# An MLP that begins on two of the first four tiles, with a shorter float64 conversion and column sums on PE

## The chip, the core and the metric

The kernel runs on one core of one Trainium2 chip. The core has five engines with their own instruction queues: PE (TensorE, matrix products), DVE (VectorE), ACT (ScalarE), POOL (GpSimd) and SP (SyncE, which here only issues DMAs). An engine takes its instructions strictly in the order in which they were written for it; between engines they wait on semaphores. The metric is the time of one execution on the device in microseconds, the median of several runs.

## The reference

Three stages follow each other on 4 x 768 = 3072 tokens.

```python
# 1. a state space model: 4 batches, 8 heads, head width 32, state 16
M = (C @ B.T) * exp(cum_i - cum_j) * causal            # in chunks, with a carried state
y = M @ x + (C @ state) * exp(cum)
# 2. an MLP; w_in [256, 2048] and w_out [2048, 256] are float64
x = relu(x @ w_in) ** 2 @ w_out
# 3. eight experts; each token goes to the one with the largest cosine to expert_emb
out[mask] = gate[mask] * (relu(x[mask] @ w1[e]) @ w2[e])   # w1[e] [256, 1024]
```

Products are taken in two float16 pieces per operand (a rounded part and the rest), so each product of the reference is three matmuls. The float64 weights are turned into float32 on the chip by integer operations on their two 32-bit words, then scaled by a power of two that comes from their size, then split into the two pieces.

## The kernel before

The 3072 tokens are 24 tiles of 128, in 6 groups of 4 tiles. Per tile the first stage is a chain: `ssm_b` (PE L655, DVE L663, POOL L671), `ssm_u` (the carried state: POOL L689, PE L694, DVE L701, POOL L707), `ssm_c` (PE L726 and L731, ACT L736), `ssm_d` (PE L746, DVE L752, ACT L759 and L762, and for the second piece DVE L771, or ACT L766 with POOL L768), and a DMA transposition (SP L776) that brings the tile to the MLP's layout.

The MLP works by `unit(u)`: group g = u // 16 and one sixteenth f = u % 16 of the 2048 hidden columns. The first product of a unit is 6 matmuls of 512 columns (four tiles at once, L896), then ReLU on ACT (L901), the square on DVE (L909) or ACT (L906), the rounded piece on ACT (L913) and the rest on DVE (L917) or POOL (L920). The second product is 12 matmuls of 256 columns (L933). All tiles of a group must have gone through the first stage before its first unit starts, and for group 0 also quarter f // 4 of w_in must be converted, scaled and split; a second product needs quarter f // 4 of w_out.

The weights: two matrices (wi = 0, 1) in four quarters of 1024 columns. For each, `top64` takes |high word| on ACT (L422) and clamps it on DVE with a running maximum (L429); `scale64` makes the scale out of the maxima (L440 to L469); `part64` builds the float32 value by one shift of 1024 columns (L480) and two passes of 1024 columns that read the raw words (L483, L486), multiplies by the scale and splits (ACT L505, then DVE L508, or POOL L514 with a scaled copy by ACT L512 or DVE L503). The scale needs the maxima of all four quarters.

After the MLP each group goes through `finish` (a transposition by DMA, the logits on PE L982) and `route` (the expert's choice, the place of each token in its expert's list: PE L1040 to L1047), and its rows are scattered to DRAM. The w1 and w2 of eight experts are loaded and split in the background (ACT L553 and L570, DVE L572). At the end run 28 `job`s, each 128 rows of one expert: a first product of 12 matmuls of 512 columns (L1256), ReLU into two pieces (ACT L1307, DVE L1309), a DMA transposition (SP L1267), a second product of 16 matmuls (L1281, L1283), the gate (ACT L1291, DVE L1294), a scatter by POOL (L1297). Jobs 13 and later use a second table of jobs, which exists only when all tokens are placed.

The order on every engine is written by a list scheduler, `weave`: each stage is a generator that yields an engine and a cost, the scheduler takes the piece that could start first by its own clock, and among nearly equal ones the one with the smallest due number (`DUE`, a table of some hundred numbers). `keep_warm` puts matmuls on zeros (L367) where its clock sees PE idle before the MLP.

## Time and profile before

| | us |
|---|---|
| median of 3 runs | 543.41 (541.89 to 543.64) |
| the profiled execution, time | 545.03 |
| its span, first to last instruction | 543.3 |
| PE busy | 506.5 (93%) |
| DVE busy | 367.2 (68%) |
| ACT busy | 319.6 (59%) |
| POOL busy | 170.1 (31%) |

Read it by stages. Up to 58 us PE works for the first stage of some nine tiles and fills the gaps with matmuls on zeros. From there to 373 us it runs the MLP with the rest of the first stage and the routing in between; from there on the jobs. PE is the engine that is nearly always busy; DVE and ACT are close to it in the first 300 us and half idle in the jobs.

### The profile page before, as it was taken

The page shows a single profiled execution, that of the slowest core. Times are in us where ns is not written, and L with a number is a line of the kernel's source. Part 1 is how long each engine was busy: PE and PEld are TensorE (multiplying, and loading weights), DVE is VectorE, ACT ScalarE, POOL GpSimd, SP SyncE. Part 2 cuts the span into 40 slices and gives each one's busy share as a digit, 9 for nine tenths or more (in the row PEclk, how much of TensorE's full clock was granted, in tenths as well). Part 3 has the DMA queues.
Part 4 walks back from the last instruction along what each step waited for, and adds up shares of the span by engine and source line. Part 5 has one row for each costly group of instructions (what it writes and reads, how often), then busy time and mean ns, then how long its engine had stood idle before and what let it go on. Part 6 is the DMA issues. An engine that isn't in the chain of part 4 may idle for free. (4 is left out here: it accounts for less than half of the span.)

```text
span 543.3 us, 11918 instructions
## 1 busy us (share of the span) xinstructions
PE 506.5 (93%) x4092; PEld 324.8 (60%) x4092; DVE 367.2 (68%) x958; ACT 319.6 (59%) x676; POOL 170.1 (31%) x182
## 2 busy tenths in 40 slices
PE   8788888999999999999998999999898898998993
PEld 6566544667776767676765766666454454554551
DVE  5988698897788798889777687765564332333330
ACT  3645679743898797989888698445422222332330
POOL 0565745536425712500140041040114121121212
PEclk9999889999999999999999999999999999999998
DMA  8933302113622334327139030203898885879751
GB/s 333 408 126 98 108 11 60 49 30 109 190 94 99 116 62 162 112 61 250 53 144 189 7 108 20 31 31 67 166 146 158 167 194 116 160 138 153 147 114 45
DMA packets 116556, 65.64 MB, mean 121 GB/s; under 512 B 105605, under 2 KB 109967, under 8 KB 113424
## 3 DMA queue, kind: packets, MB, share of 16 engines
q1 hardware_dynamic: 114000, 58.46, 43.6%
q0 software_dynamic: 2496, 6.40, 3.7%
q8 instruction: 36, 0.59, 0.4%
q14 instruction: 24, 0.20, 0.1%
HBM read 32.58 MB, written 8.13 MB: 75 GB/s over the span
## 5 line engine op out<-in xcount | busy, mean ns | idle before, releaser
L896 PE MATMUL bank<-work 128*128 128x512 f16 x576 | 142.2, 385 | 1.7 <-DVE work L909 1.5
L933 PE MATMUL bank<-work 128*128 128x256 f16 x960 | 119.2, 275 | 0.0
L933 PEld LDWEIGHTS <-work 128*128 128x128 f16 x960 | 93.3, 99 | 22.8 <-DVE work L917 0.8
L896 PEld LDWEIGHTS <-work 128*128 128x128 f16 x576 | 55.2, 99 | 53.6 <-issue 5.7
L1281 PE MATMUL bank<-wexp,work 128*128 x224 | 74.3, 379 | 6.4 <-DMA work<-work 5.8
L1256 PE MATMUL bank<-wexp,work 128*128 x336 | 76.7, 379 | 2.6 <-DMA work<-work 1.9
L1309 DVE SCALAR_TENSOR_TENSOR work<-bank,work 128x512 f16<-128x512 f32 x56 | 37.8, 689 | 52.1 <-ACT work L1307 49.1
L901 ACT ACTIVATE work<-bank 128x512 f32<-128x512 f32 x96 | 56.5, 593 | 27.5 <-PE bank L896 26.0
L1297 POOL DMA_INDIRECT out<-work x28 | 27.5, 981 | 134.4 <-DVE work L1294 80.5
L909 DVE SCALAR_TENSOR_TENSOR work<-bank,work 128x512 f32<-128x512 f32 x80 | 54.5, 685 | 15.9 <-ACT work L901 15.7
L1307 ACT ACTIVATE work<-bank 128x512 f16<-128x512 f32 x56 | 32.4, 595 | 55.5 <-PE bank L1256 29.6
L913 ACT CAST work<-work 128x512 f16<-128x512 f32 x80 | 48.7, 614 | 21.7 <-DVE work L909 18.9
L1283 PE MATMUL bank<-wexp,work 128*128 x224 | 61.0, 272 | 0.0
L920 POOL TENSOR_TENSOR work<-work 128x512 f16<-128x512 f32 x20 | 26.1, 1303 | 105.3 <-ACT work L913 92.5
L1256 PEld LDWEIGHTS <-work 128*128 128x128 f16 x336 | 32.6, 98 | 39.1 <-issue 2.1
L671 POOL TENSOR_SCALAR_AFFINE_SELECT wexp<-wexp 128x512 f32<-128x512 f32 x48 | 38.2, 795 | 54.5 <-DVE wexp L663 30.4
L917 DVE TENSOR_TENSOR work<-work 128x512 f16<-128x512 f32 x60 | 41.5, 696 | 10.2 <-ACT work L913 9.5
L1291 ACT ACTIVATE work<-bank,work 128x256 f32<-128x256 f32 x28 | 13.3, 474 | 54.7 <-PE bank L1283 51.1
L663 DVE TENSOR_TENSOR wexp<-bank,wexp 128x256 f32<-128x256 f32 x96 | 38.1, 415 | 7.7 <-PE bank L655 3.4
L1281 PEld LDWEIGHTS <-work 128*128 128x128 f16 x224 | 21.8, 98 | 35.5 <-DMA work<-work 9.6
L1294 DVE SCALAR_TENSOR_TENSOR work<-bank,work 128x256 f32<-128x256 f32 x28 | 13.5, 483 | 43.0 <-ACT work L1291 43.0
L1079 POOL DMA_INDIRECT xs<-work x24 | 29.5, 1228 | 33.4 <-DVE work L1075 10.4
(201 smaller groups left out, 759.8 us busy)
## 6 DMA issues: line engine op xcount, KB each, us to landing
work<-in_w SPq DMA_DIRECT2D x8, 1024.0 KB
wexp<-in_w SPq DMA_DIRECT2D x8, 1024.0 KB
wexp<-in_w_in SPq DMA_DIRECT2D x4, 1024.0 KB
wexp<-in_w_out SPq DMA_DIRECT2D x4, 1024.0 KB
wexp<-in_x SPq DMA_DIRECT2D x6, 512.0 KB
wexp<-in_ct SPq DMA_DIRECT2D x6, 256.0 KB
wexp<-in_bc SPq DMA_DIRECT2D x6, 256.0 KB
xs<-work SPq DMA_DIRECT2D x9, 132.0 KB
```

The costliest lines, as they stand in the source:

```text
L663: V.tensor_tensor(mv, ps.rearrange("p (a b) -> p a b", b=32), eg[:, t, n * q:n * q + n].rearrange("p h q -> p (h q)").unsqueeze(2) .to_bro ...
L671: G.affine_select(out=mm, in_=mm, pattern=[[0, 4], [1, P]], compare_op=ALU.is_ge, fill=0.0, base=0, channel_multiplier=-1)
L896: T.matmul(p, win[:, wi, kk, f * P:(f + 1) * P], x[:, xi * 2 + kk], start=(n == 0), stop=(n == 5))
L901: S.activation(r, p, AF.Relu, scale=XK)
L909: V.scalar_tensor_tensor(out=r, in0=p, scalar=XK, in1=r, op0=ALU.mult, op1=ALU.mult)
L913: S.copy(gh, r)
L917: V.tensor_tensor(gl, r, gh, ALU.subtract)
L933: T.matmul(po, gg[:, s], wout[:, wi, f], start=(f == 0 and n == 0 and k % 2 == 0), stop=(f == NF - 1 and n == 2), skip_group_check=True)
L1256: T.matmul(p, xj[i][:, xi * 2 + kk], W[:, bass.ds(e, 1), c0:c0 + 512].rearrange("p a b -> p (a b)"), start=(n == 0), stop=(n == 5))
L1281: T.matmul(po, r[:, f], W[:, bass.ds(e, 1), c0:c0 + 512].rearrange("p a b -> p (a b)"), start=(f == 0), stop=False, skip_group_check=True)
L1283: T.matmul(po[:, 0:DM], r[:, 8 + f], W[:, bass.ds(e, 1), c0:c0 + 256].rearrange("p a b -> p (a b)"), start=False, stop=(f == 7), skip_grou ...
L1309: V.scalar_tensor_tensor(out=rh[:, 1, s], in0=p, scalar=0.0, in1=rh[:, 0, s], op0=ALU.max, op1=ALU.subtract)
```

## The change

It has these parts.

- Group 0 of the MLP is no longer 16 units of 512 columns but 32 half-units, `unit0(f, hf)`, of 256 columns: half 0 takes tiles 0 and 1, half 1 tiles 2 and 3. A half waits for its own two tiles only. The rounded and rest pieces of group 0 stand where they stood before; the second products of half 0 go to bank 2, of half 1 to bank 3.
- The conversion (`conv64`) copies the high word on ACT with a factor 2^-112, shifts it on DVE, and then does two passes per half quarter (512 columns), the first into a PSUM bank, the second from it. The clamp with the running maximum is gone. The scale comes from column sums: PE multiplies a quarter, read as bfloat16, by ones (32 output rows, 2 matmuls of 512 columns per quarter), and DVE takes the maximum of the bank.
- The splits, the squares and the tiles' second pieces are shared out anew: 6 of the 8 quarters' rests on DVE (2 before) and 2 on POOL (6 before); squares on ACT: 24 of 32 halves in group 0 (8 of 16 units before), 12 of 16 units in group 1 (8 before), 32 of 64 in groups 2 to 5 (none before); the second piece of a tile's transposition on ACT and POOL for 16 of 24 tiles (2 before); the rests of group 0 on POOL for 16 of 32 halves (none before).
- In `route` four matmuls that add the running counts become one of 32 columns that reads the counts four times over.
- A job's second product may stand on PE only behind the first product of the job two later. A new kind of request, "order", keeps the order without counting as a wait in the scheduler's clock.
- Tables of the first stage use other banks; the zero matmuls have 176 columns instead of 256; `DUE` has new numbers throughout.

```diff
-XK = 2.0 ** -23
+XK = 2.0 ** -22
-DUE = dict(jm=13.1, r0=571.698, r1=-28.445, r2=3.074, r3=58.399, sv=0.3, ss=0.432, sg=0.924, g0=-0.006, g1=1, g2=0,
+DUE = dict(jm=13.1, r0=941.955, r1=-46.678, r2=-171.439, r3=67.992, sv=0.068, ss=0.348, sg=0.312, g0=-32.82, g1=1,
...
-            while th[3] is not None and th[3][0] in ("need", "mark", "due", "spawn"):
+            while th[3] is not None and th[3][0] in ("need", "order", "mark", "due", "spawn"):
...
-                    th[2] = max(th[2], marks[key])
+                    if kind == "need":
+                        th[2] = max(th[2], marks[key])
...
+    def conv64(wi, q):
         x = wides[wi][:, q]
+        xi = x.bitcast(I32)
         yield "need", ("raw", wi, q)
         yield "S", 0.95
-        S.activation(x, pair(wi, q)[:, :, 1].bitcast(F32), AF.Abs)
...
-        V.tensor_scalar(out=x, in0=x, scalar1=TINY64, scalar2=0.0, op0=ALU.max, op1=ALU.max,
-                        accum_out=mq[:, 4 * wi + q:4 * wi + q + 1])
...
+        S.activation(x, pair(wi, q)[:, :, 1].bitcast(F32), AF.Copy, scale=2.0 ** -112)
+        yield "V", 0.6, "L"
+        V.tensor_scalar(out=xi, in0=xi, scalar1=3, scalar2=None, op0=ALU.logical_shift_left)
...
+        for h in range(2):
+            T.matmul(bank[c][32 * q:32 * q + 32, :], one_b[:, 0:32],
+                     x.bitcast(BF16).rearrange("p (e w) -> p e w", w=2)[:, 512 * h:512 * h + 512, 1],
+                     start=(h == 0), stop=(h == 1), skip_group_check=True)
+        yield "mark", ("nrm", wi, q)
...
+        for h in range(2):
+            s = slice(512 * h, 512 * h + 512)
+            yield "order", ("cv", 8 * wi + 2 * q + h - 1)
+            yield "V", 0.6, (2,), "L"
+            V.scalar_tensor_tensor(out=yi, in0=pair(wi, q)[:, s, 1], scalar=-(1 << 31), in1=xi[:, s],
+                                   op0=ALU.bitwise_and, op1=ALU.bitwise_or)
+            yield "V", 0.6, (2,)
+            V.scalar_tensor_tensor(out=xi[:, s], in0=pair(wi, q)[:, s, 0], scalar=29, in1=yi,
+                                   op0=ALU.logical_shift_right, op1=ALU.bitwise_or)
+            yield "mark", ("cv", 8 * wi + 2 * q + h)
...
+    def unit0(f, hf):
+
+        cols = slice(256 * hf, 256 * hf + 256)
+        p, r = bank[f % 2][:, cols], rbuf[f % 2][:, cols]
...
+        for key in ((hr, f - 2), (hg, f - 2), ("part", 0, f // 4), ("d", 2 * hf), ("d", 2 * hf + 1)):
+            yield "need", key
...
+                T.matmul(p, win[:, wi, kk, f * P:(f + 1) * P], xT[0][:, xi * 2 + kk, cols], start=(n == 0),
+                         stop=(n == 5), skip_group_check=True)
...
+        for key in (("part", 1, f // 4), ("cv", 15), ("nrm", 1, 3), ("inv", 1)):
+            yield "need", key
...
+        for k in range(2):
+            po = bank[2 + hf][:, k * DM:k * DM + DM]
+            s = slice(k * P, (k + 1) * P)
+            for n, (gg, wi) in enumerate(((gh, 0), (gh, 1), (gl, 0))):
+                T.matmul(po, gg[:, s], wout[:, wi, f], start=(f == 0 and n == 0 and k == 0),
+                         stop=(f == NF - 1 and n == 2), skip_group_check=True)
...
-        for k in range(4):
-            T.matmul(pos[:, k * E:k * E + E], onef_s[0:1, :], base[0:1, :], start=False, stop=(k == 3),
-                     skip_group_check=True)
+        T.matmul(pos.rearrange("p (t e) -> p t e", e=E), onef_s[0:1, :],
+                 base[0:1].unsqueeze(1).to_broadcast([1, 4, E]), start=False, stop=True, skip_group_check=True)
...
+        yield "order", ("m1j", min(j + 2, JU - 1))
         yield "need", ("out", j - 2)
-        yield "need", ("m2j", j - 1)
+        yield "order", ("m2j", j - 1)
```

What the change does to the order shows at three places. First, on PE, where the MLP begins. In the kernel before L655 is the ninth tile's `ssm_b`, L746 the sixth tile's `ssm_d`, and L896 the first product of the first unit (six matmuls).

```order
L655 MATMUL bank_67<-wexp 128x128
L655 MATMUL bank_68<-wexp 128x128
L655 MATMUL bank_69<-wexp 128x128
L655 MATMUL bank_70<-wexp 128x128
L746 MATMUL bank_70<-wexp 128x128 x2
L896 LDWEIGHTS work
L896 MATMUL bank_63<-work 128x512
L896 LDWEIGHTS work
```

In the changed kernel L642 is `ssm_b`, L881 the first product of a half-unit; ahead of these rows only four tiles have their L642 and three their `ssm_d`.

```order
L881 MATMUL bank_64<-work 128x256
L881 LDWEIGHTS work
L881 MATMUL bank_64<-work 128x256
L881 LDWEIGHTS work
L881 MATMUL bank_64<-work 128x256
L881 LDWEIGHTS work
L881 MATMUL bank_64<-work 128x256
L881 LDWEIGHTS work
L881 MATMUL bank_64<-work 128x256
L642 MATMUL bank_67<-wexp 128x128
L642 MATMUL bank_68<-wexp 128x128
L642 MATMUL bank_69<-wexp 128x128
```

The first product of the first half-units thus moved ahead of five tiles' `ssm_b`. The first row of a second product (L921) comes after 138 matmuls of L881 (23 of 32 half-units) and eight tiles' `ssm_b`, and right behind the last of the 192 matmuls of L921 PE has placed ten tiles' L642, nine tiles' L718 (`ssm_c`, before L731) and seven tiles' L713 (before L726).

Second, on DVE, where the scale of w_in is made (before: L455 takes the maximum to all partitions, L465 is the scale, L480 and L483 the shift and the first pass over raw words of another quarter).

```order
L455 COPY work<-bank_67 128x1
L463 TENSOR_SCALAR work<-work 128x1
L465 TENSOR_SCALAR work<-work 128x1
L469 TENSOR_SCALAR work<-work 128x1
L276 TENSOR_SCALAR work<-work 128x1
L278 TENSOR_SCALAR work<-work 128x1
L276 TENSOR_SCALAR work<-work 128x1
L278 TENSOR_SCALAR work<-work 128x1
L480 TENSOR_SCALAR work<-work 128x1024
L663 TENSOR_TENSOR wexp<-bank_67,wexp 128x256
L483 SCALAR_TENSOR_TENSOR work<-wexp,work 128x1024
```

In the changed kernel L469 takes the maximum, L473 is the scale, L444 and L447 are the two passes over half a quarter, L496 the split of a quarter, L650 and L739 belong to the first stage (before L663 and L752).

```order
L447 SCALAR_TENSOR_TENSOR work<-wexp,bank_65 128x512
L469 TENSOR_SCALAR work<-bank_64 128x1
L472 TENSOR_SCALAR work<-work 128x1
L473 TENSOR_SCALAR work<-work 128x1
L280 TENSOR_SCALAR work<-work 128x1
L444 SCALAR_TENSOR_TENSOR bank_65<-wexp,work 128x512
L739 TENSOR_TENSOR wexp<-bank_70,wexp 128x256
L650 TENSOR_TENSOR wexp<-bank_69,wexp 128x256
L496 SCALAR_TENSOR_TENSOR work<-work 128x2x512
```

The scale's rows moved from the 77th shown row of DVE to the 57th, and the first split follows it at once. The last of the sixteen L447 is the 133rd.

Third, on DVE, jobs 10 to 15, where the second job table comes in (L1309 and L1358 end the first product of a job, two rows each; L1294 and L1343 end its second product).

```order
L1289 TENSOR_TENSOR work<-work 128x1
L1294 SCALAR_TENSOR_TENSOR work<-bank_69,work 128x256
L1289 TENSOR_TENSOR work<-work 128x1
L1294 SCALAR_TENSOR_TENSOR work<-bank_65,work 128x256
L1289 TENSOR_TENSOR work<-work 128x1
L1294 SCALAR_TENSOR_TENSOR work<-bank_69,work 128x256
L1309 SCALAR_TENSOR_TENSOR work<-bank_63,work 128x512
L1309 SCALAR_TENSOR_TENSOR work<-bank_64,work 128x512
L1309 SCALAR_TENSOR_TENSOR work<-bank_67,work 128x512
L1309 SCALAR_TENSOR_TENSOR work<-bank_68,work 128x512
```

The three second products of jobs 10, 11 and 12 stood side by side ahead of the first products of jobs 13 and 14.

```order
L1338 TENSOR_TENSOR work<-work 128x1
L1343 SCALAR_TENSOR_TENSOR work<-bank_69,work 128x256
L1358 SCALAR_TENSOR_TENSOR work<-bank_63,work 128x512
L1358 SCALAR_TENSOR_TENSOR work<-bank_64,work 128x512
L1338 TENSOR_TENSOR work<-work 128x1
L1343 SCALAR_TENSOR_TENSOR work<-bank_65,work 128x256
L1358 SCALAR_TENSOR_TENSOR work<-bank_67,work 128x512
L1358 SCALAR_TENSOR_TENSOR work<-bank_68,work 128x512
L1338 TENSOR_TENSOR work<-work 128x1
L1343 SCALAR_TENSOR_TENSOR work<-bank_69,work 128x256
```

Now first and second products take turns there, as they did before and after that place in the kernel before.

## Rows read from the trace of the kernel before

**Rows 1.** Stretches of core 0: length, each engine busy, TensorE clock, DMA share, GB/s.

```profile
0.00:58.15 58.15, 47.70 (x590) 35.04 (x591) 45.33 (x119) 30.40 (x62) 28.48 (x43) 1.00 0.65 237
58.15:100.00 41.85, 37.89 (x301) 21.25 (x300) 36.77 (x72) 32.08 (x71) 21.24 (x20) 0.92 0.18 45
100.00:200.00 100.00, 99.58 (x1086) 71.89 (x1084) 83.11 (x230) 73.41 (x177) 49.21 (x56) 1.00 0.35 100
200.00:300.00 100.00, 97.22 (x736) 66.49 (x735) 83.07 (x206) 86.38 (x179) 22.79 (x17) 0.98 0.45 133
```

**Rows 2.** Instruction groups of PE from 0 to 100 us: count, busy us, mean ns.

```profile
L896 PE MATMUL bank<-work 128*128 128x512 f16 x96 | 26.2, 414 | 1.5 <-DVE work L909 1.5
...
L655 PE MATMUL bank<-wexp 32*128 32x128 f32 x192 | 10.1, 299 | 0.8 <-DVE wexp L663 0.5 <-ACT wexp L614 0.3
L731 PE MATMUL bank<-wexp 128*32 128x128 f32 x176 | 7.1, 278 | 0.0
L726 PE MATMUL bank<-wexp 128*128 128x128 f32 x36 | 6.2, 296 | 2.0 <-POOL wexp L707 2.0
L933 PE MATMUL bank<-work,wexp 128*128 128x256 f16 x41 | 5.1, 273 | 0.0
```

**Rows 3.** PE in order of time: start us, us, instruction, count, idle before.

```profile
58.15 2.76 PE L896 MATMUL bank<-work 128*128 128x512 f16 x6
...
87.28 0.73 PE L655 MATMUL bank<-wexp 32*128 32x128 f32 x16
87.94 1.47 PE L896 MATMUL bank<-work 128*128 128x512 f16 x6
89.25 1.47 PE L933 MATMUL bank<-work,wexp 128*128 128x256 f16 x12
90.56 1.46 PE L896 MATMUL bank<-work 128*128 128x512 f16 x6
91.85 0.61 PE L726 MATMUL bank<-wexp 128*128 128x128 f32 x4
92.39 0.64 PE L731 MATMUL bank<-wexp 128*32 128x128 f32 x16
```

**Rows 4.** ACT in order of time, the first split of the weights.

```profile
52.22 2.19 ACT L505 ACTIVATE work<-work 128x1024 f16<-128x1024 f32 x2 [1.20 <-DVE work L465]
```

**Rows 5.** POOL in order of time, two halves of the split.

```profile
55.89 2.13 POOL L514 TENSOR_TENSOR work<-work 128x1024 f16<-128x1024 f32 x1
...
69.86 3.09 POOL L514 TENSOR_TENSOR work<-work 128x1024 f16<-128x1024 f32 x1
```

**Rows 6.** DVE in order of time, one subtraction of the MLP.

```profile
70.88 2.61 DVE L917 TENSOR_TENSOR wexp<-work,wexp 128x512 f16<-128x512 f32 x1
```

**Rows 7.** Instruction groups of DVE from 0 to 100 us, shapes apart.

```profile
L663 DVE TENSOR_TENSOR wexp<-bank,wexp 128x256 f32<-128x256 f32 x48 | 19.2, 415 | 2.4 <-PE bank L655 1.2 <-PE bank L446 0.6 <-ACT wexp L633 0.4
...
L429 DVE TENSOR_SCALAR_CACHE_REDUCE work<-work 128x1024 f32<-128x1024 f32 x8 | 9.7, 1212 | 0.9 <-ACT work L422 0.9
...
L909 DVE SCALAR_TENSOR_TENSOR work<-bank,work 128x512 f32<-128x512 f32 x8 | 5.5, 682 | 1.8 <-ACT work L901 1.8
...
L480 DVE TENSOR_SCALAR work<-work 128x1024 int32<-128x1024 int32 x6 | 4.1, 684 | 0.1
```

**Rows 8.** Instruction groups of ACT from 0 to 100 us, shapes apart.

```profile
L505 ACT ACTIVATE work<-work 128x1024 f16<-128x1024 f32 x5 | 5.4, 1100 | 1.2 <-DVE work L465 1.2
...
L906 ACT ACTIVATE work<-work 128x512 f32<-128x512 f32 x7 | 4.4, 628 | 0.0
...
L736 ACT COPY wexp<-bank 128x256 f32<-128x256 f32 x11 | 4.1, 370 | 8.9 <-PE bank L731 7.2 <-PE bank L655 1.1 <-DVE wexp L663 0.4
```

**Rows 9.** PE in order of time, the expert counts of one group.

```profile
262.20 1.05 PE L1044 MATMUL bank<-work 1*128 1x8 f32 x8
```

**Rows 10.** What PE waited for from 373.5 us: total us, times, longest.

```profile
PE bank L1281 <- DMA work<-work: 5.8, 9, 1.4
PE bank L1256 <- DMA work<-work: 1.9, 1, 1.9
```

More of the change, by code (lines that the diff above doesn't have):

```diff
@@ L343, in weave @@
             cost = th[3][1]
-            if eng == "T" and ("m1", 1) not in marks:
+            if eng == "T" and ("h10", 1) not in marks:
                 keep_warm((s - free[eng]) * (DUE["warm"] if s > 6 else DUE["cold"]))
@@ L354, in weave @@
                 th[2] = s + 4.0
-            elif th[3][-1] == "L" or eng == "G":
-                free["L"] = s + cost
-            elif type(th[3][-1]) is tuple:
-                for b in th[3][-1]:
-                    held[b, eng] = th[2] + XLAT[eng]
+            else:
+                if th[3][-1] == "L" or eng == "G":
+                    free["L"] = s + cost
+                for what in th[3][2:]:
+                    if type(what) is tuple:
+                        for b in what:
+                            held[b, eng] = th[2] + XLAT[eng]
             th[3] = next(th[1], None)
@@ L435, in scale64 @@
+    def scale64(wi, inv_ap):
         sc, m = scw[:, wi:wi + 1], mx[:, wi:wi + 1]
-        mi = mxr[:, wi:wi + 1].bitcast(I32)
         for q in range(4):
-            yield "need", ("nrm" if wi == 1 and DUE["nw"] else "top", wi, q)
-        yield "V", 0.2
-        V.tensor_reduce(out=m, in_=mq[:, 4 * wi:4 * wi + 4], op=ALU.max, axis=AX.X)
-        row = bank[4][0:1, 288:416]
+            yield "need", ("nrm", wi, q)
+        c = 2 * wi + 1
+        yield "V", 0.6, (c,)
+        V.tensor_reduce(out=m, in_=bank[c], op=ALU.max, axis=AX.X)
+        row = bank[c][0:1, 0:P]
@@ L452, in scale64 @@
-        yield "T", 0.1, (4,)
-        T.matmul(bank[4][:, 288:289], onef_s[0:1, :], m[0:1], start=True, stop=True, skip_group_check=True)
-        yield "V", 0.1, (4,)
-        V.tensor_copy(m, bank[4][:, 288:289])
-        if wi == 1 and DUE["nw"]:
-            yield from scale_bits(m.bitcast(I32), sc.bitcast(I32), inv_ap.bitcast(I32), 205)
-            inverses(inv_ap.bitcast(I32), 49)
-            yield "mark", ("scale", wi)
-            yield "mark", ("inv", wi)
-            return
-        yield "V", 0.2
@@ L471, in scale64 @@
+        inverses(hi, -14)
         yield "mark", ("inv", wi)
@@ L644, in ssm_b @@
         yield "need", ("m", t - 1)
-        bs = [(4 if g else 2) + r for r in range(4)]
-        sc = [bank[bs[r]][:, (0, 256)[g > 0 and r > 1]:][:, 0:256] for r in range(4)]
+        bs = [4 + r for r in range(4)]
+        sc = [bank[bs[r]][:, (0, 256)[r > 1]:][:, 0:256] for r in range(4)]
         yield "need", ("ct", g)
@@ L883, in unit @@
         r = rbuf[u % 2]
-        if g == 0:
-            gh, gl = (first[:, 1024 * f + 512 * i:1024 * f + 512 * i + 512] for i in range(2))
-        else:
-            gh, gl = ghb[u % 3], glb[u % 3]
-        for key in (("m1", u - 1), ("r", u - 2), ("part", 0, f // 4), ("eg", 0)):
+        gh, gl = ghb[u % 3], glb[u % 3]
+        if u < NF + 2:
+            for key in (("hr0", u - 2), ("hg0", u - 2)):
+                yield "need", key
+        yield "order", ("m1", u - 1)
+        for key in (("r", u - 2), ("part", 0, f // 4), ("eg", 0)):
             yield "need", key
@@ L921, in unit @@
         yield "mark", ("gl", u)
-        yield "due", DUE["m0"] + DUE["m1"] * u if u < NF else due(u + 2)
-        for key in (("m2", u - 1), ("part", 1, f // 4), ("m", 3)):
-            yield "need", key
+        yield "due", due(u + 2)
+        yield "order", ("m2", u - 1)
         if f == 0:
@@ L1249, in job @@
             yield "need", ("jr%d" % q, j - 2)
-            yield "need", ("m1j", j - 1)
+            yield "order", ("m1j", j - 1)
             yield "T", 1.296, (hb[j % 2][q],)
@@ L1455, in tile_ssm_mlp_moe @@
         th += [(d + DUE["ob"], ssm_b(t)), (d + DUE["ou"], ssm_u(t)), (d + DUE["oc"], ssm_c(t)), (d, ssm_d(t))]
-    for u in range(NF * NGRP):
+    for f in range(NF):
+        for hf in range(2):
+            th.append((due(f) + hf * DUE["uh"], unit0(f, hf)))
+    for u in range(NF, NF * NGRP):
         th.append((due(u), unit(u)))
```

181 lines of the change are left out of this document (100 added, 81 removed).

## Prediction

> **What bounds the kernel now.** I read the stretches first, then the groups of PE in the first 100 us, then each engine in order of time around the start of the MLP, and last what PE waits for in the jobs. The stretches [rows 1] show two regimes. From 100 us on PE has no room: 99.58 busy of 100, then 97.22, while DVE is at 83 and ACT at 73 and 86. So whatever PE has not done by 100 us is paid later one to one, and the question is how much more it gets done before. Ahead of that, PE's 47.70 of 58.15 is not work for the most part: the zero matmuls are in it. The MLP begins at 58.15 [rows 3]. What released it stands on two other engines: the first split of w_in starts on ACT at 52.22, behind a wait for the scale (L465) [rows 4], and POOL ends its half of that split at 55.89 + 2.13 = 58.02 [rows 5]. The tiles are not late then; the weights are. DVE, which makes the scale, is busy 45.33 of the 58.15 [rows 1], most of the rest being the wait for the first data.
>
> What PE has done by 100 us, by the groups [rows 2] at the pitch of the consecutive rows (start to start, [rows 3]): 96 / 6 = 16 first products at 1.30 = 20.8; 41 / 12 = 3.4 second products at 1.31 = 4.5; 192 / 16 = 12 tiles of L655 at 0.66 = 7.9; 176 / 16 = 11 of L731 at 0.6 = 6.6; 36 / 4 = 9 of L726 at 0.54 = 4.9. Together 44.7. Tables and small matmuls are left out, as they are nearly the same on both sides.
>
> **The head.** In the changed order PE has, with the last second product of group 0, 16 + 16 units, ten tiles of the first kind, nine of the second and seven of the third: 20.8 + 21.0 + 6.6 + 5.4 + 3.8 = 57.6, less about 1.5 for two or three tiles' small matmuls that it has not done yet. That is 57.6 - 1.5 - 44.7 = 11.4 more than the kernel before has at 100 us, and this one, without gaps from there, has it at 111.4. The gain of the head is 111.4 minus the time T at which the changed kernel has it.
>
> T is the start of the first second product plus what PE has behind it: 32 second half-products at 0.655 = 21.0, the last nine first ones at 0.65 = 5.9, and 4.6 for two tiles: 31.5, and 0.5 for small waits. A half has half the columns, and twelve matmuls of 256 columns take 1.31 [rows 3], as six of 512 do, so the cut costs PE nothing.
>
> The first second product needs the whole conversion of w_out, which is DVE's. By the order, DVE has up to the last L447: 32 passes of 512 columns at 0.68 (L909 is the nearest form, also with a PSUM operand) = 21.8; 8 shifts at 0.68 = 5.4; 4 splits of 1024 columns at twice 0.68 = 5.5; two maxima of 512 columns 1.4; 50 rows of 256 columns at 0.415 = 20.8; some 33 rows of one column, which I put at 0.15, 5. Sum 60 [rows 7]. The clamps with the maximum, 8 x 1.21 = 9.7, are gone from it [rows 7]; the two passes cost the same columns as before. From data at about 6 us and at the 85 to 87% that DVE held since then, that is 75; where neighbours overlap by a tenth it is 68. ACT comes to the same: ahead of the 23rd half it has, from the first split on, ten rows of 1024 columns at 1.10 and 79 of 256 columns or fewer at 0.37, 40 us [rows 8]; the first split is at about 32, since DVE needs only 24 us of rows ahead of its own half of it (13 passes, 4 shifts, 18 rows of 256 columns, the maximum, the split): 6 + 24 / 0.85 = 34, and the first product at 35 instead of 58.15. So 72 for the first second product, between 65 (nothing idle) and 80. PE fits into it: 23 half-products are 15, four tiles about 10, of the 37 us between 35 and 72. T = 72 + 31.5 + 0.5 = 104, and the gain 7.4; at the ends 14.4 and -0.6. The column sums are 16 matmuls of 512 columns, 0.22 each by 1.30 / 6, 3.5 in all, in stretches where PE waits anyway; were that cover gone, they cost half of it, the half behind 35 us.
>
> The transpositions of tiles 0 and 1 must have landed too. On SP they now stand among the loads of w_out, the second one behind the last quarter, whose loads filled the DMA engines to 65% over the first 58 us [rows 1]. They need not be there before 34, so I charge nothing; late by some us they would delay first products that PE has time for.
>
> **The routing.** The four count matmuls are eight rows of 1.05 us [rows 9]; one of 32 columns leaves two rows, at 0.13 each. That is 0.75 less in each of six groups, five of them in the stretches without gaps: 3.7, bounds 2 (if a wider row takes twice as long and more) and 4.5.
>
> **The jobs.** PE waits 5.8 us in nine second products for their transposition, and 1.9 once ahead of a first product [rows 10]. The order shows that second products stood two jobs later before already, except for jobs 10 to 12; the new condition therefore changes one place. There it takes away a pile-up of three, but job 13's first product, which needs the second table, now stands in front of two second products that covered its rows' way: 2 lost at worst, 3 gained at best. I take 1.0 gained.
>
> **ACT in the middle.** 36 more squares of 512 columns at 0.63 [rows 8] and 14 more tile copies at 0.37 put 28 us on ACT between 100 and 370 us, and take as much from DVE. ACT's 40 idle us from 100 to 300 [rows 1] hide it if they come at the right time. I charge 1.0, bounds 0 and 14.
>
> **Sum.** 7.4 + 3.7 + 1.0 - 1.0 = 11.1 less than the profiled execution's 545.0, that is 533.9. That execution lies 1.6 above the median of the runs, so I predict 543.4 - 11.1 = 532.3.
>
> **Rivals.**
> *The conversion is late, and the head gains nothing.* POOL now takes 16 subtractions of group 0 and half a dozen tile pieces inside the stretch in which DVE converts. One row speaks for it: a DVE subtraction that starts at 70.88 takes 2.61 [rows 6], where a row of 512 columns takes 0.68 [rows 7], beside a POOL subtraction that itself takes 3.09 instead of 2.13 [rows 5]. Were 22 DVE rows held for a POOL row of 256 columns, a quarter of 2.13, 12 us would be added and the first second product comes at 84; from 79.4 on nothing is gained in the head. Against it: the two big POOL splits that made this worst go from six to two. With the routing's 3.7 that gives 541 to 545, say 543.
> The Trainium skill, page SBUF — State Buffer, section Who interferes with whom, says that a DVE instruction with two SBUF inputs and a GpSimd instruction that reads SBUF exclude each other, and the second waits for the whole of the first. The pair at 70 us agrees with it. By that rule the first pass of the conversion is exposed, and the second, whose intermediate lies in PSUM, is not, so half of the 32 passes would be safe; the sum would keep 72 rather than go to 84.
>
> *ACT becomes the bound of the middle: slower.* From 200 to 300 us it is at 86.38 already [rows 1]; its share of the new squares and copies there is about 10, which leaves 4 free. If PE then waits for rounded pieces behind w1 and w2 work, about half of the 28 us lands on the path: 532 + 14 = 546, and all of it would give 560. It decides once ACT shows 97 or more of 100. Against it: the order spreads the experts, and ACT has room from 300 us on.
>
> *The head goes better.* DVE and ACT have a backlog that waits for nobody and run without a pause: first second product at 65, T 97, head 14.4: 525; with the jobs' best case 522.
>
> **Numbers.** Forecast as above, 525 to 541: 0.67. Late conversion: 0.13. ACT in the middle: 0.11. Better head: 0.09. The range is 522 to 544: it takes in the better head and the late conversion, and leaves out ACT's case. Runs of this kernel differ by about 0.3%, so less than that (541.8 to 545.0) counts as the same. Faster: 0.67 + 0.09 + 0.05 of the late conversion = 0.81. Same: 0.06 of it and 0.02 of ACT's case, 0.08. Slower: 0.02 and 0.09, 0.11.
>
> **What would show it.** The first half-product near 35 us and the first second product near 72; group 0's last second product near 104; from there PE without gaps; DVE's rows of two SBUF inputs near 0.7 in the head; the count matmuls two rows per group. Wrong it would be if the second products start behind 80, if PE waits for ACT between 150 and 300 us, or if job 13 waits several us in front of the second products of jobs 11 and 12.

## The result, and the profile after

| | us |
|---|---|
| changed kernel, median of 18 runs | 538.96 (532.99 to 542.37) |
| kernel before, median of 18 runs beside them | 544.04 (541.77 to 547.41) |
| ratio | 0.989, 95% interval 0.9865 to 0.9915 |
| profiled execution, time | 540.01 |
| its span | 538.3 |

By the ratio the change takes 5.9 us off (4.6 to 7.3). The forecast was 11.1: the sign is right, the size about half. (The ratio and all verdicts below leave disturbed runs out; the medians are over all runs.)

The stretches of the changed kernel, over the same boundaries as before [rows 1] (columns as there; the engines are PE, PE's weight loads, DVE, ACT and POOL):

```profile
0.00:58.15 58.15, 47.46 (x505) 33.60 (x506) 43.90 (x106) 40.68 (x88) 28.45 (x42) 0.94 0.64 228
58.15:100.00 41.85, 39.45 (x410) 32.06 (x410) 29.44 (x76) 32.42 (x90) 23.68 (x32) 0.92 0.21 65
100.00:200.00 100.00, 98.68 (x1039) 70.18 (x1037) 76.60 (x231) 86.80 (x210) 46.12 (x58) 1.00 0.42 116
200.00:300.00 100.00, 97.84 (x846) 67.03 (x844) 73.38 (x190) 89.00 (x194) 33.44 (x32) 1.00 0.33 97
```

PE is busy about as long as before, but the granted clock is 0.94 in the first stretch, where it was 1.00. ACT has more to do and DVE less: ACT 89.00 of 100 from 200 to 300 us instead of 86.38, DVE 73.38 instead of 83.07, and PE is at 97.84, where it was at 97.22. PE in order of time, the rows that answer to [rows 3], first half-products (L881) and in the last row the first second product (L921):

```profile
36.38 1.69 PE L881 MATMUL bank<-work 128*128 128x256 f16 x12
...
57.27 3.06 PE L881 MATMUL bank<-work 128*128 128x256 f16 x24
...
61.88 0.81 PE L881 MATMUL bank<-work 128*128 128x256 f16 x6 [1.33 <-DVE work L895]
...
67.23 4.54 PE L881 MATMUL bank<-work 128*128 128x256 f16 x24
...
77.13 2.13 PE L921 MATMUL bank<-work,wexp 128*128 128x256 f16 x18
```

The first half-product stands at 36.38 (forecast 35); the first split had started on ACT at 34.20. The first second product comes at 77.13 instead of 72, and the last of the 192 matmuls of L921 starts at 108.9 instead of 104. The row at 67.23 says why to look further: 24 matmuls take 4.54 us, while 24 of them took 3.06 at 57.27. The granted clock (the column behind POOL), in four stretches of the head:

```profile
18.00:26.00 8.00, 7.60 (x68) 5.30 (x65) 6.11 (x16) 3.78 (x10) 5.16 (x6) 0.60 1.04 398
26.00:64.00 38.00, 30.64 (x334) 20.71 (x334) 34.67 (x78) 34.49 (x84) 21.41 (x27) 0.99 0.32 98
64.00:71.00 7.00, 7.00 (x49) 5.07 (x50) 4.64 (x11) 4.92 (x11) 3.81 (x5) 0.51 0.09 19
71.00:109.00 38.00, 37.81 (x414) 32.25 (x412) 22.93 (x66) 24.58 (x71) 20.61 (x27) 1.00 0.28 78
```

From 18 to 26 and from 64 to 71 us PE runs at 0.60 and 0.51, for most of it at the lower level of 1.2 GHz. Ahead of the second fall PE had been idle a good part of the time:

```profile
48.00:52.00 4.00, 2.51 (x23) 1.50 (x23) 3.62 (x10) 3.26 (x9) 2.07 (x4) 1.00 0.00 0
52.00:56.00 4.00, 3.02 (x34) 2.28 (x33) 2.93 (x8) 3.87 (x11) 3.43 (x4) 1.00 0.02 4
56.00:60.00 4.00, 3.88 (x44) 3.14 (x45) 3.69 (x11) 3.13 (x9) 2.04 (x3) 1.00 0.16 33
60.00:64.00 4.00, 1.84 (x22) 1.20 (x19) 4.00 (x8) 3.92 (x14) 1.34 (x2) 1.00 0.00 0
```

2.51, 3.02, 3.88 and 1.84 busy of 4 us each. During the fall PE is what the others wait for: DVE in order of time has a gap,

```profile
72.09 0.42 DVE L739 TENSOR_TENSOR wexp<-bank,wexp 128x256 f32<-128x256 f32 x1 [3.42 <-POOL wexp L676]
...
76.17 0.68 DVE L447 SCALAR_TENSOR_TENSOR work<-wexp,bank 128x512 int32<-128x512 int32 x1
```

3.42 us ahead of L739, whose matmuls (L733) stood behind those 24 and started at 71.61 (the POOL row that it names ended at 72.07, in a queue behind subtractions that waited for the same first products). The last pass of the conversion (L447) ends at 76.85, 0.3 ahead of the first second product. In every trace of the changed kernel and its variants below, the first second product starts within 0.3 us of the end of that pass, so the end of the conversion does set it.

### The profile page after: what moved, and what is told of

Same layout as the page of the kernel before. It is cut to its first block, busy times and chain, and to the rows that moved or that the text cites. A ratio compares the mean times of both kernels' runs of the same rounds, so it can differ in the third digit from the quotient of the medians.

```text
span 538.3 us, 12038 instructions
## 1 busy us (share of the span) xinstructions
PE 500.4 (93%) x4105; PEld 327.0 (61%) x4105; DVE 334.0 (62%) x907; ACT 351.2 (65%) x774; POOL 179.9 (33%) x208
## 5 line engine op out<-in xcount | busy, mean ns | idle before, releaser
L981 PE MATMUL bank<-work 128*128 128x256 f16 x960 | 116.5, 273 | 1.2 <-DVE work L966 0.7
L945 PE MATMUL bank<-work 128*128 128x512 f16 x480 | 114.2, 379 | 0.6 <-DVE work L958 0.5
L981 PEld LDWEIGHTS <-work 128*128 128x128 f16 x960 | 92.0, 98 | 21.3 <-DVE work L966 1.5
L1330 PE MATMUL bank<-wexp,work 128*128 x224 | 75.5, 383 | 6.1 <-DMA work<-work 5.3
L1303 PE MATMUL bank<-wexp,work 128*128 x336 | 77.3, 380 | 3.1 <-DMA work<-xs 1.7
L945 PEld LDWEIGHTS <-work 128*128 128x128 f16 x480 | 46.0, 99 | 44.5 <-issue 1.5
L1358 DVE SCALAR_TENSOR_TENSOR work<-bank,work 128x512 f16<-128x512 f32 x56 | 37.9, 690 | 48.7 <-ACT work L1356 41.9
L1332 PE MATMUL bank<-wexp,work 128*128 x224 | 61.6, 275 | 0.0
L950 ACT ACTIVATE work<-bank 128x512 f32<-128x512 f32 x80 | 46.9, 591 | 17.0 <-PE bank L945 16.2
L1303 PEld LDWEIGHTS <-work 128*128 128x128 f16 x336 | 32.9, 98 | 40.3 <-issue 2.4
L969 POOL TENSOR_TENSOR work<-work 128x512 f16<-128x512 f32 x20 | 27.6, 1380 | 85.3 <-ACT work L962 85.3
L966 DVE TENSOR_TENSOR work<-work 128x512 f16<-128x512 f32 x60 | 45.3, 756 | 17.4 <-ACT work L962 14.5
L1340 ACT ACTIVATE work<-bank,work 128x256 f32<-128x256 f32 x28 | 13.3, 474 | 52.9 <-PE bank L1332 51.1
L658 POOL TENSOR_SCALAR_AFFINE_SELECT wexp<-wexp 128x512 f32<-128x512 f32 x48 | 36.0, 752 | 31.6 <-DVE wexp L650 23.3
L1330 PEld LDWEIGHTS <-work 128*128 128x128 f16 x224 | 22.0, 98 | 35.1 <-DMA work<-work 8.3
L650 DVE TENSOR_TENSOR wexp<-bank,wexp 128x256 f32<-128x256 f32 x96 | 38.1, 415 | 5.1 <-PE bank L642 1.6
L1343 DVE SCALAR_TENSOR_TENSOR work<-bank,work 128x256 f32<-128x256 f32 x28 | 13.5, 483 | 43.6 <-ACT work L1340 43.6
L955 ACT ACTIVATE work<-work 128x512 f32<-128x512 f32 x44 | 27.8, 631 | 0.5
```

Source lines behind the costliest of these rows:

```text
L650: V.tensor_tensor(mv, ps.rearrange("p (a b) -> p a b", b=32), eg[:, t, n * q:n * q + n].rearrange("p h q -> p (h q)").unsqueeze(2) .to_bro ...
L658: G.affine_select(out=mm, in_=mm, pattern=[[0, 4], [1, P]], compare_op=ALU.is_ge, fill=0.0, base=0, channel_multiplier=-1)
L945: T.matmul(p, win[:, wi, kk, f * P:(f + 1) * P], x[:, xi * 2 + kk], start=(n == 0), stop=(n == 5))
L950: S.activation(r, p, AF.Relu, scale=XK)
L966: V.tensor_tensor(gl, r, gh, ALU.subtract)
L981: T.matmul(po, gg[:, s], wout[:, wi, f], start=(f == 0 and n == 0 and k % 2 == 0), stop=(f == NF - 1 and n == 2), skip_group_check=True)
```

## The experiments

Each was timed beside the kernel before, both on the same chip; a ratio is against that. Not all experiments ran on the same chip. "Clock lost" is the sum of (1 - granted clock) x length over stretches of 2 us.

**The kernel before again,** unedited.

> The kernel before once more, for the granted clock of its single runs. The changed kernel's 18 runs spread from 533.0 to 542.4 us and go with their mean clock (0.994 to 0.970): about 0.7 us of time for each us of full clock lost. Clock theory (the head fell short of its forecast by some 5 us because PE fell to 1.2 GHz where DVE waited for it): the kernel before has a narrower spread, its clock within 0.983 to 0.992, its times within 541.5 to 547.5. Rival (the spread of clocks is that of any kernel of this shape, and the change is not to blame): clocks from 0.97 to 0.995 here too, and times that follow them by the same slope.

Measured: 543.82, ratio 0.9997 (0.9966 to 1.0027), clocks from 0.979 to 0.997, times 540.9 to 547.5. Over all runs of these experiments with a clock on record, 85 of this kernel, and the 24 of the changed one, mean time and clock are 543.4 at 0.989 and 537.9 at 0.983, and the slope (least squares) is 3.1 and 3.6 us for 0.01 of clock. So both expectations are half right: the kernel before depends on its clock nearly as much, but its times spread less (standard deviation 1.8 us against 3.1), and the changed kernel runs at 0.006 less, about 2 us. On the two fitted lines, at equal clock (0.990), the kernels are 7.7 us apart.

**More zeros.** The scheduler issues zero matmuls for each us in which its own clock sees PE idle. Two edits, alone and together:

```diff
-warm=4.8, cold=4.799
+warm=5.8, cold=5.8
```
```diff
-            if eng == "T" and ("h10", 1) not in marks:
+            if eng == "T" and ("h20", 0) not in marks:
```

> 5.8 instead of 4.8 zero matmuls per idle us that the scheduler sees ahead of the MLP (118 instead of 99), so that 176 columns cover as much of it as 256 did before; all else stands where it stood. Clock theory: the fall to 1.2 GHz at 18 to 26 us goes or is shorter, DVE's waits for PE between 21 and 29 us (2.3 us) go, mean clock up by 0.006, time 1 to 3 us less than the changed kernel (536 to 538). Rival (what sets the head is DVE's and POOL's contention, not PE's clock): time within 1 us of the changed kernel, whatever the clock does.

> Zero matmuls go on in PE's idle time after the first products have begun, up to the first second product (128 instead of 99); all else stands where it stood. Clock theory: the fall to 1.2 GHz at 64 to 71 us goes, DVE's wait of 3.4 us at 69 goes with it, first second product at 73 to 74 instead of 77.1, last one of group 0 at 105 to 106 instead of 108.9, time 3 us less than the changed kernel (535 to 537). Rival (contention sets the conversion): first second product stays at 77, time the same or up to 3 us more, which is what the 29 zeros cost in PE's queue.

> Both additions of zero matmuls together: 5.8 per idle us, and on until the first second product (157 instead of 99). Clock theory: mean clock at 0.988 to 0.993 as in the kernel before, first second product at 71 to 73, time 534 to 537, so 2 to 4 us under the changed kernel and 7 to 9 under the kernel before. Rival (the zeros stand in PE's way): first second product at 75 or later, 538 or more.

| | median, us | ratio | first and last second product of group 0 |
|---|---|---|---|
| 5.8 per us | 537.51 | 0.9872 (0.9820 to 0.9924) | 73.2, 105.0 |
| on to the second product | 536.37 | 0.9879 (0.9829 to 0.9929) | 71.5, 103.3 |
| both | 533.40 | 0.9812 (0.9778 to 0.9846) | 73.2, 105.0 |

The second products come earlier in all three traces, as the clock theory said. In the times, each edit alone is within 3 us of the changed kernel, with an interval that overlaps its own. Together they give the lowest median here, with an interval below that of the 18 runs (0.9865 to 0.9915), though not below that of the six further runs of the changed kernel that follow. The trace of the second edit has no fall in the head:

```profile
18.00:26.00 8.00, 6.64 (x93) 4.60 (x93) 6.68 (x16) 5.43 (x13) 5.78 (x8) 1.00 1.05 402
26.00:64.00 38.00, 31.86 (x355) 22.14 (x347) 35.64 (x81) 34.79 (x83) 21.30 (x28) 1.00 0.37 98
64.00:71.00 7.00, 6.58 (x89) 5.29 (x88) 6.59 (x17) 6.94 (x22) 4.75 (x7) 1.00 0.09 19
71.00:109.00 38.00, 38.00 (x419) 31.79 (x418) 23.05 (x71) 24.95 (x72) 19.33 (x25) 1.00 0.37 110
```

Part of that is luck. The second edit changes nothing on PE ahead of 37 us, so its zeros can't have taken away the fall at 18 to 26 us; that fall was absent in this execution, and its second products came earlier than the expectation (73 to 74, 105 to 106) for that reason too.

**The changed kernel again,** unedited.

> The changed kernel once more, for a second trace and more runs with their clocks. Clock theory: where this trace shows no fall to 1.2 GHz between 18 and 71 us, the first second product is at 71 to 73 us and the last one of group 0 at 103 to 105; where it shows one there, they are later by 0.7 to 0.9 us for each us of full clock lost. Rival (the head differs from run to run for other reasons): the first second product at 76 us or later without a fall.

Measured: 536.28, ratio 0.9857 (0.9813 to 0.9901). Its trace has one fall in the head, 20 to 31 us, and none at 64, though the program is the same: the falls differ from one execution to the next. First and last second product are at 75.5 and 107.3. The traces with this head in the same order, sorted by the clock lost ahead of the last second product:

| clock lost, us | first, last second product | trace |
|---|---|---|
| 6.8 | 77.1, 108.9 | changed kernel |
| 6.8 | 76.7, 108.5 | four counts (below) |
| 5.1 | 76.0, 107.8 | value in SBUF (below) |
| 5.1 | 76.4, 108.2 | condition on the jobs removed (below) |
| 5.1 | 75.5, 107.3 | changed kernel again |
| 5.1 | 75.2, 107.0 | squares back on DVE (below) |
| 1.7 | 73.2, 105.0 | 5.8 per us; both |
| 0 | 71.5, 103.3 | zeros on |

About 0.8 us for each us of clock lost (least squares 0.78), and 103.3 without any; at the same 5.1 the heads still lie up to 1.2 us apart. The table by itself would allow that a delay from elsewhere left PE idle and brought both, the lost clock and the late head. The zeros speak against that, as they do nothing but occupy PE: the three traces with more of them have the last second product at 103.3 to 105.0, the six without at 107.0 to 108.9. So the theory holds for the head, with one trace for each edit.

**The control: the same zeros in the kernel before.** From the first MLP product on they go to a bank that is free until the first second product.

```diff
-warm=4.8, cold=4.799
+warm=5.8, cold=5.8
-            if eng == "T" and ("m1", 1) not in marks:
+            if eng == "T" and ("m2", 0) not in marks:
-            T.matmul(bank[1 if ("eg", 0) in marks else 6][:, 256:512], idle_s[:, 0:P], idle_s, start=True, stop=True,
+            T.matmul(bank[3 if ("m1", 0) in marks else 1 if ("eg", 0) in marks else 6][:, 256:512], idle_s[:, 0:P], idle_s, start=True, stop=True,
```

> The kernel before with both additions of zero matmuls (5.8 per idle us, and on until the first second product; 212 instead of 162), all else in its place: the control for the run that had them in the changed kernel and took 533.4 us. Theory that the zeros give back only what the change itself put at risk: within 1 us of the kernel before (542 to 544). Rival (any kernel of this shape gains from them): 3 us or more under it, 541 or less, and then the change is worth less at equal clock than 533.4 against 542.4 says.

Measured: 538.90, ratio 0.9940 (0.9913 to 0.9966), 3.3 us less. The rival holds. Its trace and that of the kernel before over three stretches, first with zeros:

```profile
56.00:62.00 6.00, 6.00 (x62) 3.83 (x61) 4.18 (x12) 3.78 (x10) 6.00 (x6) 1.00 0.36 94
74.00:80.00 6.00, 5.95 (x69) 3.81 (x67) 5.97 (x12) 6.00 (x12) 3.13 (x6) 1.00 0.11 22
290.00:300.00 10.00, 10.00 (x87) 7.29 (x85) 8.91 (x26) 8.74 (x15) 1.16 (x1) 1.00 0.38 120
```

```profile
56.00:62.00 6.00, 6.00 (x58) 3.74 (x58) 2.73 (x10) 3.17 (x9) 5.29 (x4) 0.72 0.26 87
74.00:80.00 6.00, 5.85 (x42) 3.12 (x45) 5.77 (x14) 5.11 (x11) 2.14 (x3) 0.72 0.09 18
290.00:300.00 10.00, 7.36 (x56) 4.69 (x54) 6.64 (x22) 7.04 (x16) 1.16 (x1) 0.84 1.19 196
```

The kernel before had lost clock too, at 56 to 62, 74 to 80 and 290 to 300 us. The zeros reach only the first two of these stretches: the last of them starts at 81.3 us. In the third one PE was idle 2.6 us in the kernel before, for another reason,

```profile
294.27 0.31 PE L982 MATMUL bank<-work 128*128 128x8 f16 x6 [1.64 <-DMA work<-work]
295.53 0.31 PE L982 MATMUL bank<-work 128*128 128x8 f16 x6 [0.96 <-DMA work<-work]
```

two waits for the transposition in `finish`; in the trace with zeros PE doesn't wait there at all, and why is not shown. The last second product of group 0 starts 2.4 to 3.5 us earlier with zeros (134.3 instead of 136.7 and 137.8 in the two traces without), and that is about what the time gained; the traces also differ by some 5 us between there and the first job, where no zeros stand.

So the zeros are no repair of this change alone. With them on both sides the change is worth 0.994 against 0.9812, 7.0 us (4.6 to 9.3), or 5.5 by the two medians; without, 5.9 (4.6 to 7.3). The two are not told apart.

**The early start undone.**

```diff
-        for key in ((hr, f - 2), (hg, f - 2), ("part", 0, f // 4), ("d", 2 * hf), ("d", 2 * hf + 1)):
+        for key in ((hr, f - 2), (hg, f - 2), ("part", 0, f // 4), *(("d", t) for t in range(4))):
```

> Undoes the early start alone: a half-unit waits for all four tiles of group 0, as a unit did before. First half-product near 48 instead of 36. Theory that the conversion of w_out on DVE sets the first second product (so that PE has room for the first products): first second product stays at 76 to 78, time 0 to 2 us more than the changed kernel. Rival (the early start itself is what gained in the head): the 12 us reach the second products at least by half, first one at 83 or later, time 5 us or more above the changed kernel.

Measured: 556.14, ratio 1.0226 (1.0185 to 1.0267), 18 us above the changed kernel. The first half-product came at 50.9, but the first second product at 68.1 and the last at 106.2, earlier than in the changed kernel. PE stood idle for the conversion ahead of the first one:

```profile
PE bank L921 <- DVE work L447: 2.9, 1, 2.9
```

Neither theory foresaw that: the size is the rival's, its way isn't. The scheduler made another order out of the condition, in which fewer other rows stand ahead of the second products: with the last of them PE has done eight tiles' `ssm_b` (L642), seven tiles' L718 and five tiles' L713, against ten, nine and seven in the changed kernel. Counted at the forecast's pitches, it has done the same rows only at 117.9 us, against 109.2, though the two traces lost about as much clock up to there (6.3 and 6.8 us). So the head is some 9 us later at equal work. The stretch in which that shows:

```profile
106.00:112.00 6.00, 3.95 (x69) 2.86 (x70) 4.57 (x20) 3.86 (x13) 2.43 (x4) 1.00 0.93 311
112.00:123.00 11.00, 10.94 (x103) 7.20 (x104) 7.11 (x29) 7.60 (x21) 5.95 (x10) 0.53 0.50 61
123.00:126.00 3.00, 3.00 (x20) 1.64 (x18) 2.64 (x8) 2.27 (x6) 0.00 (x0) 1.00 0.83 259
```

From 106 us on PE has only first-stage work in front of it, for which it waits (3.95 busy of 6), and then runs at 0.53 for 11 us. From the last second product of group 0 to the first job it takes 273.3 us, against 260.0; the jobs take 175.8 against 169.4, with three falls of the clock where the changed kernel has one (not counting the one at the very end, which every trace has). The order follows the condition here, so this tells what the start on two tiles is worth in this order with these due numbers (18 us), not what it is worth after a new tuning.

**The clamps put back** (the price alone; the maximum changes no value).

```diff
+        V.tensor_scalar(out=x, in0=x, scalar1=-3e38, scalar2=0.0, op0=ALU.max, op1=ALU.max,
+                        accum_out=mq[:, 4 * wi + q:4 * wi + q + 1])
         V.tensor_scalar(out=xi, in0=xi, scalar1=3, scalar2=None, op0=ALU.logical_shift_left)
```

> Puts back the price of the clamps alone: DVE runs a maximum over each quarter of 1024 columns again (8 rows of 1.21 us, 9.7 in all, values unchanged), in the place ahead of the shift; all instructions keep their order. Theory of the forecast (DVE's rows set the first second product): first second product 8 to 11 us later than the changed kernel's 71.5 to 77, so 80 to 88, and the time 6 to 10 us more (544 to 549). Rival (DVE has slack in the head, the clamps were hidden): first second product within 3 us of the changed kernel's, time within 2 us of its 539.

Measured: 547.04, ratio 1.0057 (1.0026 to 1.0087), 9 us above the changed kernel; first second product at 85.0, last at 116.8. As the theory had it, DVE's rows set the second products. But 12.0 us of clock were lost ahead of that (18 to 34 and 48 to 68 us), 5.1 more than in the changed kernel; at 0.8 each some 4 of the 8 us go with the clock, an estimate, and some 4 are left for the 9.7 us of rows themselves.

**The value between the passes in SBUF.**

```diff
-            V.scalar_tensor_tensor(out=yi, in0=pair(wi, q)[:, s, 1], scalar=-(1 << 31), in1=xi[:, s],
+            V.scalar_tensor_tensor(out=xi[:, s], in0=pair(wi, q)[:, s, 1], scalar=-(1 << 31), in1=xi[:, s],
...
-            V.scalar_tensor_tensor(out=xi[:, s], in0=pair(wi, q)[:, s, 0], scalar=29, in1=yi,
+            V.scalar_tensor_tensor(out=xi[:, s], in0=pair(wi, q)[:, s, 0], scalar=29, in1=xi[:, s],
```

> The value between the two conversion passes stays in SBUF (in place) instead of PSUM, as it did before the change; sizes and order are the same. Theory that a DVE row of two SBUF inputs is held by POOL's rows: the second pass (L447), 0.68 us in all 16 now, spreads as the first one does (0.68 to 1.56, mean 0.84), 2 to 3 us more in the head, first second product 2 to 3 us later, time 1 to 3 us more. Rival (the first pass is long for another reason, such as its strided read of the raw words): the second pass stays at 0.68 and the time within 1 us of 539.

Measured: 538.22, ratio 0.9914 (0.9879 to 0.9949). The second pass (line; min, median, max ns; first and last start), in the changed kernel and then here:

```profile
L447 DVE SCALAR_TENSOR_TENSOR work<-wexp,bank x16: 670/680/687, 12.5 to 76.2; 128x512 int32<-128x512 int32 x16
```

```profile
L447 DVE SCALAR_TENSOR_TENSOR work<-wexp,work x16: 675/774/1152, 12.5 to 74.9; 128x512 int32<-128x512 int32 x16
```

670 to 687 ns with a PSUM operand, 675 to 1152 with two from SBUF: the sixteen rows took 13.3 us instead of 10.9. That is the first theory, 2.4 us of DVE. The rival, the strided read, is answered by the first pass of the changed kernel, which has that read in all its rows: the three that no POOL row overlapped took 689 to 701 ns, the thirteen that one did 683 to 1559. The time doesn't show the 2.4 us: it is +1.3 us in the ratio, inside the interval, and the first second product at 76.0 with 1.7 us less clock lost, which is where 0.8 each would put it or 0.3 above.

**Four counts.**

```diff
-        T.matmul(pos.rearrange("p (t e) -> p t e", e=E), onef_s[0:1, :],
-                 base[0:1].unsqueeze(1).to_broadcast([1, 4, E]), start=False, stop=True, skip_group_check=True)
+        for k in range(4):
+            T.matmul(pos[:, k * E:k * E + E], onef_s[0:1, :], base[0:1, :], start=False, stop=(k == 3),
+                     skip_group_check=True)
```

> Undoes the routing alone: four count matmuls per group again (eight rows of PE instead of two), order kept. Theory of the forecast: 0.75 us per group, five groups on PE's path, 3.7 us more than the changed kernel (542 to 543), and from group 0's last second product to the first job 263 to 264 us instead of 259.9 to 261.7. Rival (PE has small waits there now that hide it): under 1.5 us more, PE's idle time in that stretch falls by as much as its work grows.

Measured: 540.43, ratio 0.9926 (0.9892 to 0.9959), 2.0 us above the changed kernel's ratio, intervals overlapping. From the last second product to the first job it takes 262.3 us instead of 260.0. That stretch took 258.1 to 261.7 in the traces above and below that have its order, and most of the difference between them is PE's wait for the transposition ahead of the logits (L1030), 2.0 to 5.6 us in all; in this trace that wait is 2.9, and the traces with 2.6 to 3.2 took 259.1 to 260.0. So some 2.3 to 3.2 us are the counts'. A group's rows of the changed kernel:

```profile
251.22 0.40 PE L1091 MATMUL bank<-work 1*128 1x32 f32 x2
251.56 0.26 PE L1094 MATMUL bank<-work 128*128 128x8 f16 x4
```

From start to the next start the two rows take 0.34. In the kernel before, behind the row of [rows 9] at 262.20, the next one was

```profile
263.19 0.26 PE L1047 MATMUL bank<-work 128*128 128x8 f16 x4
```

so that the eight took 0.99. That is 0.65 per group, 3.2 in five, the forecast's theory with a smaller price.

**The condition on the jobs removed.**

```diff
-        yield "order", ("m1j", min(j + 2, JU - 1))
```

> Undoes the condition on the jobs alone: a second product no longer has to stand behind the first product two jobs later; the second products of jobs 9 to 12 stand in two pairs again. Theory of the forecast: 1 us more than the changed kernel, from the first job to the end 170.5 instead of 169.5. Rival (the condition costs: job 13's first product, which waits for the second table, now holds up two second products): 1 to 2 us less; no wait of 1.7 us ahead of a first product at 442.

Measured: 538.55, ratio 0.9852 (0.9802 to 0.9902): 2 us less than the changed kernel's ratio, inside the intervals; nothing is told apart. What PE waits for in the jobs, first the changed kernel, then without the condition (L1303 is a first product in both, L1330 and L1329 a second one):

```profile
PE bank L1330 <- DMA work<-work: 5.3, 5, 2.5
PE bank L1303 <- DMA work<-xs: 1.7, 1, 1.7
...
PE bank L1303 <- DVE work L1343: 1.4, 1, 1.4
```

```profile
PE bank L1329 <- DMA work<-work: 8.3, 7, 2.0
PE bank L1303 <- DVE work L1342: 1.8, 1, 1.8
...
PE bank L1303 <- DMA work<-xs: 0.2, 1, 0.2
```

In the traces of the changed kernel's order of the jobs the second products wait 5.2 to 7.0 us for their transposition, so the condition takes 1.3 to 3.1 us of waits off them, and job 13's first product waits 1.4 to 1.7 instead of 0.2 in front of them. The jobs of this one trace took 171.3 us against 168.5 to 170.1 with the condition, which points the other way than the ratio; its time, 541.25, is the second longest of its six runs.

**The squares back on DVE.**

```diff
-s1=0.75, s2=0.5
+s1=0.5, s2=0
```

> Undoes the squares' shares from group 1 on: ACT does 8 of 16 in group 1 and none in groups 2 to 5, as before, and DVE the others; the scheduler's order follows (the head up to the last second product of group 0 hardly moves). Theory of the forecast (36 more squares on ACT cost about 1 us): the time 0 to 2 us under the changed kernel. Rival (ACT near its bound costs several us in the middle): 3 us or more under it. Third (DVE is the engine that needs the relief): 2 us or more above it.

Measured: 544.55, ratio 1.0008 (0.9972 to 1.0044), 6 us above the changed kernel. By its number the third theory holds; its cause, that DVE needed the relief, does not show in the middle. From 200 to 300 us:

```profile
200.00:300.00 100.00, 98.10 (x839) 67.10 (x839) 79.22 (x200) 77.21 (x167) 30.48 (x33) 0.98 0.35 104
```

ACT is down to 77.21, DVE up to 79.22, and PE is as busy as before (98.10). From the last second product of group 0 to the first job it took 261.8, against 260.0 and 259.1 in the two traces of the changed kernel, with one fall of the clock there (at 240 us) that those don't have; the rest of the 6 us came in the jobs, 173.6 against 169.4 and 169.0, with two falls of the clock there instead of one. Why the jobs fell more often with these shares stays open.

## Why the prediction was right in sign and half in size

The sum, by the profiled executions (545.03 - 540.01 = 5.0): head 111.4 - 108.9 = 2.5 (forecast 7.4); from there to the first job 260.0 against 373.5 - 111.4 = 262.1, so 2.1 (forecast 3.7 - 1.0 = 2.7); jobs 169.4 against 169.8, so 0.4 (forecast 1.0). The 111.4 is the forecast's estimate of equal work and not a row of the trace, and the last two stretches differ by 3.6 and 1.6 us between traces of the same order, so the 2.1 and the 0.4 are no clearer than that.

*The head: the mechanism right, T mis-sized.* The start at 35 (36.4), DVE's rows as what sets the second products (clamps: +8 us, half of them with more clock lost), the first second product at 72 and T = 104 hold in the one trace where PE keeps its clock: 71.5 and 103.3. The 32 us from the first to the last second product came as forecast in every trace of this order (31.8). The step that failed is that T was worked out at full clock on one side, while the 111.4 of the other side came from a trace that had lost clock. The view was there: [rows 1] shows 0.92 from 58 to 100 us, and the forecast gave it no price. In the changed kernel's trace PE falls at 18 and at 64 us, the second time after waits for DVE, and while it is slow DVE waits for it, 3.42 us in one piece. The 4.9 us between 104 and 108.9 are that, by 6.8 x 0.8 = 5.4. The kernel before pays too: held warm, it has its first second product at 85.8 us instead of 88.1 and 89.25, and by the forecast's pitches it has the rows of 111.4 some 3.5 us sooner, at 107.9. Against 103.3 that leaves the head 4.6 us at full clock on both sides, an estimate from one trace each, instead of 7.4.

*The late conversion, the rival of 0.13.* A result between the forecast and that rival could look like it; it is not. DVE's groups of the changed kernel up to the end of the conversion, the first pass, the second one and the subtractions (columns as in [rows 7]):

```profile
L444 DVE SCALAR_TENSOR_TENSOR bank<-wexp,work 128x512 int32<-128x512 int32 x16 | 13.5, 844 | 0.0
...
L447 DVE SCALAR_TENSOR_TENSOR work<-wexp,bank 128x512 int32<-128x512 int32 x16 | 10.9, 679 | 0.4
L903 DVE TENSOR_TENSOR wexp<-work,wexp 128x256 f16<-128x256 f32 x9 | 5.9, 668 | 0.8 <-ACT wexp L900 0.8
```

The first pass, of two SBUF operands, took 2.6 us more than the second, of one; the subtractions took 668 ns instead of the 415 that rows of 256 columns take with an operand from PSUM [rows 7]. The forecast looked for 0.7 us in rows of two SBUF inputs; the first pass took 0.84. That cost is real but small against the 12 us of the rival, and without clock loss the conversion was in time. The Trainium skill, page SBUF — State Buffer, section Who interferes with whom, has a DVE instruction of two SBUF inputs contend with a GpSimd instruction that reads SBUF. The two rows of L447 above agree with it, 670 to 687 ns with an operand from PSUM and 675 to 1152 without.

*The routing.* 3.7 was worked out from busy times, 1.05 - 0.26; matmuls overlap, and by starts it is 0.65 per group, 3.2. Undone, it gave 2.0 in the time, with intervals that overlap, and 2.3 to 3.2 in the stretch.

*The jobs.* 1.0 forecast, nothing told apart: both things named there happened, 1.3 to 3.1 us fewer waits of the second products and 1.2 to 1.5 more ahead of job 13; what is left of them in the time is not shown.

*ACT in the middle.* The sign of the term failed. The forecast charged 1.0 for 28 us more on ACT and gave nothing for 28 us less on DVE, though both stood in [rows 1] at 83 to 86 of 100. Undone, the share costs 6 us, some 2 of them in the middle and 4 in the jobs; that they come of DVE's load is not shown. The rival of 0.11, ACT as the bound, is refuted: at 89.00 of 100, PE waited 0.2 us for ACT between 109 and 370 us.

*Two readings on the way.* PE's 47.70 busy us up to 58.15 were not zeros for the most part: the 162 zero matmuls were busy 23.9 us, half of it. And the 0.3% by which runs of the kernel before were said to differ came from three runs; twelve further ones lie between 540.9 and 547.5, 1.2%.

## What to carry to other kernels

Work out a gain in a stretch from two times at the same clock: read the granted clock of the stretch on both sides, and where PE's work is moved ahead of what it needs from other engines, ask how often PE will now stand still and what waits for it while it is slow. Take more than one trace of each side, since the falls differ between executions of the same program. Take matmul costs from start to start, not from busy times. When work goes from one busy engine to another, price both ends.

## What the runs showed of the hardware

The runs of one kernel spread by 10 us (533.0 to 543.4 in 24), and that goes with the granted clock, 3.6 us for 0.01 of its mean. With 50 more matmuls on zeros the kernel before took 3.3 us less (0.9940); with 58 the changed one took 4.2 less than in its 18 runs (0.9812 against 0.989) and 2.4 less than in its six later ones (0.9857), the last with intervals that overlap; its median of 533.40 is the lowest here. A DVE pass over 512 columns kept 0.68 us in all sixteen cases with one operand in PSUM, and spread to 1.15 with both in SBUF, where POOL rows overlapped it.
